# A shorter first transfer of wq: 2,048 of its columns instead of 4,096

## The chip, the cores and the metric

The kernel runs on one core of one Trainium2 chip. The time is device microseconds of one execution, taken as the median of several runs; lower is better. One further execution is recorded by the hardware profiler, and all profile lines come from that one.

## The reference

One decode step for two sequences: a layer norm, attention over the last 2,048 positions of a key and value cache, and a dense layer with a squared ReLU beside it, all added to the input.

```python
# x [2,1,576]; wq [576,4096]; wo [4096,576]; w1 [576,4608]; w2 [4608,576]; caches [2,16,8192,128]; bf16
xn = _layernorm(x)
# A: 32 query heads of 128 on 16 key/value heads, window W = 2048
q = (xn @ wq) -> [2,32,1,128]
scores = einsum("bhqd,bhkd->bhqk", q, k[:, :, Sk-W:]) * 128**-0.5
o = einsum("bhqk,bhkd->bhqd", softmax(scores), v[:, :, Sk-W:])
a = o.reshape(2, 1, 4096) @ wo
# B
h = relu(xn @ w1 + b1); b = (h * h) @ w2 + b2
return x + a + b
```

## The kernel before

**What is loaded.** About 53.6 MB come from HBM: wq (4.5 MiB), eight units of keys and eight of values (2 MiB each; a unit `u` is four key/value heads of one sequence), w1 (5,184 KB), wo (4,608 KB) and w2 in five pieces. All of them are issued from SyncE's queue (SP), in the order in which the program lists them. The biases, x and the output's first half are issued from ScalarE (ACT).

**The layout of the big weights.** `issue_flat` (L115) reads a weight as one flat row of numbers and gives each of the 128 partitions an equal, contiguous piece. For wq a piece is 18,432 columns: 9 blocks of `LQ` = 2,048, one block for each `t` in `range(NH)`, `NH` = 9. The tuple `cuts` says at which columns the load is cut into several transfers; all write the same tile. The before-kernel cuts wq at column 4,096 (L131), and so the first transfer holds the blocks t = 0 and 1, the second t = 2 to 8. A transfer is one stretch of memory on each of the 128 partitions: 8 KB and 28 KB per partition.

**The query projection.** `q_rows` (L232) runs over t = 0 to 8 and four column groups g, one matmul each (36 in all, recorded under L93, the helper `matmul`), into the PSUM tile `q_ps`. Block t of wq is needed by the four matmuls of t. `q_ps` is cleared by VectorE (DVE) first (L225), and the matmuls' other operand `xnT` comes out of the layer norm. `q_place` (L240) then copies `q_ps` to `qrow` (half on DVE, half on ACT), transposes it on TensorE (PE, `qT_ps`) and spreads it into `qz`.

**The units.** `transposes(u, g)` turns the keys on PE (recorded under L96) and copies them to `kT` (ACT and DVE in turn); `scores` multiplies `kT` with `qz`; `softmax(u)` follows. Keys and values share a pool of six buffers (`kvpool`), so a load of unit u waits until an earlier unit's buffer has been read. `step(u)` also does the value product `pv` of unit u - 2. The order of work on PE is that of the program (`keep_in_program_order`).

**The order of loads on SP.** wq (two transfers), k0, k1, v0, k2, v1, k3 ahead of everything; v2 after unit 0; k4 after step 1; then a k and a v per step, w1 after step 4; v6 and v7 after step 5. wo waits for the buffer `wbig`, which w1 holds until `mlp_h` (the dense layer's first half, L357) has read it; the five pieces of w2 (`w2a`, `w2b`, three into `w2c`) follow wo. The loads k2 and v1 also wait for an earlier transfer to have landed, as the wait table shows (SP L105 waits for wq twice, 8.0 us the longest).

**The end.** PE adds wo, w2a, w2b and w2c into `out_ps` as they land; three matmuls into `spin_ps` stand between w2b and w2c and are not read. `fin_sb` is copied out and stored from two queues.

Of the kernel before, what the change touches and what calls it, by code (L numbers as in the profile page):

```python
# [16 lines left out]
def kernel(  # L17
# [91 lines left out]
    def load_k(u):  # L109
        issue_kv(k_tiles, A_k_cache, u, "k")  # L110
# [4 lines left out]
    def issue_flat(w, name, cuts=()):  # L115
        n = w.shape[0] * w.shape[1] // P
        tl = wbig.tile([P, NH * L1], BF16, tag="wbig", name=name)
        w_p = w.rearrange("r n -> (r n)").rearrange("(p l) -> p l", p=P)
        for lo, hi in zip((0,) + cuts, cuts + (n,)):
            nc.sync.dma_start(out=tl[:, lo:hi], in_=w_p[:, lo:hi])  # L120
        return tl
# [6 lines left out]
    nc.vector.memset(eps_t[:], 1e-5)  # L128
    warm = const.tile([B, 2], F32, name="warm")
    nc.scalar.activation(out=warm[:, 0:1], in_=eps_t[:], func=ACT.Sqrt)  # L130
    wq_sb = issue_flat(A_wq, "wq", (4096,))  # L131
    load_k(0)
    load_k(1)
    load_v(0)
# [376 lines left out]
```

## Time and profile before

| what | value |
|---|---|
| time, median of 3 runs | 133.66 us (133.63 to 133.71) |
| time of the profiled execution | 133.6 us |
| its span, first to last instruction | 131.7 us |
| PE busy | 84.6 us (64%) |
| DVE busy | 63.1 us (48%) |
| ACT busy | 46.6 us (35%) |
| HBM read | 53.62 MB, 407 GB/s over the span |
| DMA queue of SP | 3,604 packets, 95.6% of 16 engines' span |
| mean granted TensorE clock | 0.883 |

The profile divides the span into 40 slices of 3.3 us; a digit is the busy share in tenths. A row of the chain of waits tells, followed back from the last instruction, what released each step; a DMA in it lasts from its issue to its landing, so time in which it stood in the queue behind other transfers is in its figure. A window row gives each engine's busy time in a stretch with the number of instructions, the granted PE clock (1.00 is full), the mean busy share of the 16 DMA engines, and GB/s. A packet's time is not cut exactly at a window's border, so a DMA share a little above 1 can stand there.

### The profile page before, as it was taken

To read this page: it belongs to the slowest core of one execution; us is meant where nothing else is said; L and a number is where in the kernel's file an instruction comes from. 1 tells how busy PE (TensorE), PEld (TensorE's weight loads), DVE (VectorE), ACT (ScalarE), POOL (GpSimd) and SP (SyncE) were. 2 spreads that over 40 slices of the span, in tenths; PEclk is the share of its full clock that TensorE was granted. 3 is DMA by queue.
4 is the path that set the end of the run, shared out by engine and by line. 5 is a ranking of instruction groups with operands and counts; after the bars stand their busy time and mean duration, and the time that the engine had idled before them with its cause. 6 is when DMAs were issued, how large, how long until landed. Compare 5 with 4: busy or idle time off the path is not lost.

```text
span 131.7 us, 2025 instructions
## 1 busy us (share of the span) xinstructions
PE 84.6 (64%) x818; PEld 46.3 (35%) x818; DVE 63.1 (48%) x176; ACT 46.6 (35%) x68; POOL 4.2 (3%) x14
## 2 busy tenths in 40 slices
PE   0040767985599687699687797003919974629782
PEld 0010236553346353345353353002507631205341
DVE  6760034555447677457677496400073487560000
ACT  6700019497255185265085283200015452000101
POOL 2000000010100100100100100100010001000000
PEclk9999999999779999859999999955586899655799
DMA  4999999999999999999999999999999989899970
GB/s 118 480 419 420 418 443 418 448 418 423 445 413 438 423 443 428 413 458 413 443 423 411 458 490 403 408 431 428 413 443 418 504 381 504 382 416 403 400 286 1
DMA packets 3643, 53.74 MB, mean 408 GB/s; under 512 B 418, under 2 KB 563, under 8 KB 819
## 3 DMA queue, kind: packets, MB, share of 16 engines
q1 hardware_dynamic: 3604, 53.61, 95.6%
q8 instruction: 6, 0.10, 0.3%
q10 hardware_dynamic: 30, 0.02, 0.0%
q14 instruction: 3, 0.02, 0.0%
HBM read 53.62 MB, written 0.00 MB: 407 GB/s over the span
## 4 chain that ended last, share of the span: by engine, by line
DMA 74%; PE 15%; ACT 5%; issue 1%; SPq 1%; DVE 1%; ACTq 0%; DVEq 0%
DMA w<-in_B_w_dram 24%; DMA w2c<-in_B_w_dram 23%; DMA k<-in_A_k_cache_dram 17%; DMA wq<-in_A_wq_dram 10%; PE kT_ps L96 5%; PE h_ps L93 3%; ACT kT L273 3%; PE q_ps L93 2%; PE sc_ps L93 2%; PE o_ps L93 1%; PE out_ps L93 1%; ACT L305 1%; SPq L120 1%; DVE qrow L241 1%; ACT qrow L241 0%
## 5 line engine op out<-in xcount | busy, mean ns | idle before, releaser
L96 PE MATMUL kT_ps<-ident_f,k 128*128 128x128 f32 x256 | 39.0, 295 | 6.7 <-DMA k<-in_A_k_cache_dram 4.2
L273 ACT COPY kT<-kT_ps 128x1024 bf16<-128x1024 bf16 x32 | 31.8, 1012 | 15.3 <-PE kT_ps L96 15.3
L96 PEld LDWEIGHTS kT_ps<-ident_f,k 128*128 128x128 f32 x256 | 29.3, 149 | 21.8 <-issue 7.4
L275 DVE COPY kT<-kT_ps 128x1024 bf16<-128x1024 bf16 x32 | 21.8, 682 | 6.4 <-PE kT_ps L96 5.9
L93 PE MATMUL sc_ps<-kT,qz 128*32 128x512 bf16 x128 | 9.8, 384 | 6.1 <-DVE kT L275 5.5
L305 ACT ACTIVATE p<-sc_ps,bias 128x512 bf16<-128x512 f32 x8 | 5.5, 687 | 21.5 <-DVE gown L301 21.4
L93 PE MATMUL o_ps<-v,pT 128*32 128x512 bf16 x128 | 12.2, 466 | 0.0
L93 PE MATMUL h_ps<-w,xnT 128*4 128x288 bf16 x72 | 4.5, 442 | 8.8 <-DMA w<-in_B_w_dram 8.8
L93 PEld LDWEIGHTS <-xnT 128*4 128x4 bf16 x108 | 3.5, 117 | 18.3 <-issue 15.3
L336 DVE SCALAR_TENSOR_TENSOR o<-o_ps,in_s,o 128x128 f32<-128x128 f32 x24 | 8.2, 344 | 0.4
L308 DVE STREAM_TRANSPOSE pT<-p 128x512 bf16<-128x512 bf16 x8 | 5.7, 709 | 5.6 <-ACT p L305 5.6
L376 DVE TENSOR_TENSOR hrow<-t 100x1152 bf16<-100x1152 f32 x2 | 2.6, 1354 | 10.5 <-ACT t L374 10.5
L93 PE MATMUL q_ps<-wq,xnT 128*4 128x512 bf16 x36 | 4.2, 622 | 5.4 <-DMA wq<-in_A_wq_dram 4.0
L294 DVE TENSOR_REDUCE m<-sc_ps 128x1 f32<-128x512 f32 x8 | 5.5, 691 | 3.4 <-PE sc_ps L93 3.4
L93 PE MATMUL op_ps<-o,of_h 128*32 128x129 f32 x16 | 3.4, 299 | 4.6 <-DVE o L336 4.6
L298 POOL PARTITION_ALL_REDUCE gmax<-m x8 | 2.9, 365 | 92.2 <-DVE m L296 92.2
L93 PEld LDWEIGHTS <-qz 128*32 128x32 bf16 x128 | 2.0, 94 | 9.9 <-DVE kT L275 7.6
L334 DVE TENSOR_SCALAR o<-o_ps,in_s 128x128 f32<-128x128 f32 x8 | 2.7, 343 | 5.3 <-PE o_ps L93 5.3
L96 PE MATMUL pro_ps<-ident,xn_sb 2*128 2x2 bf16 x5 | 0.9, 181 | 6.8 <-DVE xn_sb L171 6.5
L241 ACT CAST qrow<-q_ps 100x512 bf16<-100x512 f32 x1 | 0.6, 585 | 12.1 <-DVE qrow L241 12.1
L463 ACT COPY pre_sb<-pre_ps 34x288 f32<-34x288 f32 x1 | 0.4, 393 | 12.6 <-PE pre_ps L93 12.6
L93 PE MATMUL out_ps<-wo,ws 128*2 128x288 bf16 x32 | 4.0, 441 | 1.1 <-DVE ws L352 1.1
(76 smaller groups left out, 61.4 us busy)
## 6 DMA issues: line engine op xcount, KB each, us to landing
k<-in_A_k_cache_dram SPq DMA_DIRECT2D x8, 2048.0 KB, 25.6
v<-in_A_v_cache_dram SPq DMA_DIRECT2D x8, 2048.0 KB, 22.8
w<-in_B_w_dram SPq DMA_DIRECT2D x1, 5184.0 KB
wo<-in_A_wo_dram SPq DMA_DIRECT2D x1, 4608.0 KB
wq<-in_A_wq_dram SPq DMA_DIRECT2D x1, 3584.0 KB, 12.9
w2a<-in_B_w_dram SPq DMA_DIRECT2D x1, 2592.0 KB
w2b<-in_B_w_dram SPq DMA_DIRECT2D x1, 1296.0 KB, 29.2
wq<-in_A_wq_dram SPq DMA_DIRECT2D x1, 1024.0 KB, 4.8
```

Of the source, the lines that this page charges most:

```text
L93: tc.keep_in_program_order(nc.tensor.matmul(*a, **k))
L96: tc.keep_in_program_order(nc.tensor.transpose(*a, **k))
L241: cp(out=qrow[:, k * QW:(k + 1) * QW].rearrange("p (i a d) -> p i a d", a=2, d=Dh), in_=q_ps[0:RB, k * QW // 2:(k + 1) * QW // 2].rearrang ...
L273: nc.scalar.copy(out=kT, in_=kT_ps[:])
L275: nc.vector.tensor_copy(out=kT, in_=kT_ps[:])
L294: nc.vector.tensor_reduce(out=m1[:], in_=sc_ps[:], axis=AX.X, op=ALU.max)
L298: nc.gpsimd.partition_all_reduce(gmax[:], m2[:], channels=P, reduce_op=ReduceOp.max)
L305: nc.scalar.activation(out=p_sb[:], in_=sc_ps[:], func=ACT.Exp, bias=bias[:, 0:1], scale=scale, accum_out=o1[:, Dh:Dh + 1])
L308: nc.vector.transpose(out=pT[:].rearrange("p j r -> p (j r)"), in_=p_sb[:])
L334: nc.vector.tensor_scalar(scalar1=in_s[:, 0:1], scalar2=None, op0=ALU.mult, **kw)
L336: nc.vector.scalar_tensor_tensor(scalar=in_s[:, k:k + 1], in1=o1[:, 0:Dh], op0=ALU.mult, op1=ALU.add, **kw)
L376: nc.vector.tensor_tensor(out=h4[:, :, k * HB:(k + 1) * HB], in0=t4, in1=t4, op=ALU.mult)
```

## The change

One number: the column at which wq's load is cut.

```diff
     warm = const.tile([B, 2], F32, name="warm")
     nc.scalar.activation(out=warm[:, 0:1], in_=eps_t[:], func=ACT.Sqrt)
-    wq_sb = issue_flat(A_wq, "wq", (4096,))
+    wq_sb = issue_flat(A_wq, "wq", (2048,))
     load_k(0)
     load_k(1)
```

The first transfer is 128 x 2,048 elements (512 KB, 4 KB per partition) and the second 128 x 16,384 (4,096 KB, 32 KB per partition). The number of transfers, their order on SP and every instruction of the other engines are the same in both kernels; what each matmul of `q_rows` has to wait for is not.

## The prediction

> **What bounds the kernel now.** I read the slices first, to see whether any engine is full all the time:
>
> ```profile
> PE   0040767985599687699687797003919974629782
> DMA  4999999999999999999999999999999989899970
> GB/s 118 480 419 420 418 443 418 448 418 423 445 413 438 423 443 428 413 458 413 443 423 411 458 490 403 408 431 428 413 443 418 504 381 504 382 416 403 400 286 1
> ```
>
> The 16 DMA engines are full from the second slice to the last but two; PE has holes everywhere. Next the chain of waits, of which these are the long pieces (start us, length us, what):
>
> ```profile
> 1.18 12.89 DMA wq<-in_A_wq_dram
> 14.08 0.04 issue
> 14.12 3.18 PE q_ps L93 x28
> ...
> 31.95 22.43 DMA k<-in_A_k_cache_dram
> ...
> 59.41 31.63 DMA w<-in_B_w_dram
> ...
> 96.95 30.81 DMA w2c<-in_B_w_dram
> 127.75 0.04 issue
> 127.80 1.36 PE out_ps L93 x18
> ```
>
> The chain names `q_ps`, but the three later DMA pieces are queue time. The key load issued at 31.95 moves 2 MiB, which at the 431 GB/s shown below takes 2.097/0.431 = 4.9 us, and lands after 22.4: for more than 17 us it stood behind others. So what lies ahead of 31.95 in this chain need not set the end. What sets it is the sum of bytes, from the start of the flow (about 2.5 us) to the last landing near 128, and then 1.4 us of PE and the store.
>
> Last the projection itself on PE (timeline), then the unit after which PE is first held up again by a load:
>
> ```profile
> 9.10 1.02 PE L93 MATMUL q_ps<-wq,xnT 128*4 128x512 bf16 x8 [1.37 <-DVE q_ps L225]
> 14.12 3.16 PE L93 MATMUL q_ps<-wq,xnT 128*4 128x512 bf16 x28 [4.00 <-DMA wq<-in_A_wq_dram]
> ...
> 35.05 1.97 PE L96 MATMUL kT_ps<-ident_f,k 128*128 128x128 f32 x8 [1.52 <-DMA k<-in_A_k_cache_dram]
> ```
>
> The first 8 matmuls (t = 0 and 1) wait for DVE's clearing of `q_ps`, not for wq, whose first transfer landed 4.8 us after its issue at 0.73, near 5.5. The other 28 wait 4.0 us for the second transfer. At 35.05 PE has been idle for 1.52 us until k2 landed.
>
> **The change part by part.**
>
> *Matmuls moved behind the second landing.* The first transfer now holds t = 0 alone: 4 matmuls run at 9.10, and 32 instead of 28 after 14.08. The row gives 3.18/28 = 0.114 us each, so 4 more are 0.45 us. `q_ps` is complete near 17.75 instead of 17.30, and `qrow`, `qz`, unit 0 and unit 1 follow that much later. What hides it: PE's 1.52 us of idle before k2, which shrinks to about 1.07. Late behind it are two loads that wait for buffers: v2 (issued at 24.19) and k4 (31.95). Ahead of v2 the queue holds wq and six units, 4.72 + 6 x 2.097 = 17.3 MB, which at 0.431 MB per us from 2.5 us on last until 42.6. So 18 us of cover stand against 0.45. Later loads have similar cover: no load of values took less than 19.9 us from issue to landing for its own 4.9. The last that waits for PE is wo, issued at 95.62 after the dense layer; that layer starts on w1's landing (91.04, PE idle for 8.8 us ahead of it), and k7, v6, v7 still stand behind w1, 3 x 4.9 us, so until about 105.7. Cost on the end: 0. If the cover were gone: 0.45.
>
> *The bytes at another cut.* Both kernels move the same bytes in the same number of rows. The trace has no 4 KB row, so I take the rate per busy share (GB/s divided by the DMA share) from windows in which one row length rules:
>
> ```profile
> core 0: us, PE busy (x) PEld busy (x) DVE busy (x) ACT busy (x) POOL busy (x), PEclk, DMA share, GB/s
> 3.50:4.50 1.00, 0.00 (x0) 0.00 (x0) 1.00 (x5) 0.97 (x3) 0.00 (x0) 1.00 1.03 434
> 7.00:13.00 6.00, 1.57 (x11) 0.53 (x12) 1.58 (x7) 0.00 (x0) 0.00 (x0) 1.00 1.02 441
> 20.00:60.00 40.00, 32.21 (x267) 18.82 (x265) 23.22 (x54) 22.30 (x31) 1.46 (x4) 0.91 1.01 431
> 82.00:90.00 8.00, 0.25 (x2) 0.08 (x1) 1.76 (x5) 0.78 (x2) 0.36 (x1) 0.75 0.94 402
> 127.40:128.00 0.60, 0.45 (x6) 0.17 (x5) 0.00 (x0) 0.00 (x0) 0.00 (x0) 1.00 0.42 162
> ```
>
> wq's 8 KB rows: 434/1.03 = 421. Its 28 KB rows: 441/1.02 = 432. w1's 40.5 KB rows: 402/0.94 = 428. The last pieces of w2c, rows of 2.25 and 1.125 KB (288 and 144 KB over 128 partitions): 162/0.42 = 386. Before, wq costs 1.049/0.421 + 3.670/0.432 = 2.49 + 8.50 = 10.99 us. After, 0.524 MB at 386 to 421 is 1.36 to 1.25, and 4.194 MB at 432 (32 KB lies between 28 and 40.5) is 9.71: together 10.96 to 11.07. That is -0.03 to +0.08; 4 KB stands about midway between the two ends, and I take +0.02.
>
> *The start of the flow.* Before the first byte lands, a packet of each engine is under way; a row of 8 KB on each of 16 engines is 131 KB, 0.31 us at 421, and one of 4 KB half that. If the first row has to be read whole before it is written, the flow starts 0.15 us earlier: -0.15 to 0. Against it: the first transfer drains 0.524/0.421 = 1.25 us earlier, and the second must be ready by then. From windows of half a microsecond the DMA share is 0.37 at 2.0 to 2.5, 0.73 to 3.0 and 0.93 to 3.5, so transfers issued at 0.73 flow after some 1.3 to 2.3 us. The second is issued at about 1.15 and would flow from 2.4 to 3.4; the first now ends near 5.1 - 1.25 = 3.85. So the queue does not run dry, with 0.4 us in hand. If it did, the ramp would be lost again: 0.5 x (0.63 + 0.27 + 0.07) = 0.48 us. So -0.15 to +0.48; nearest to the rows is no bubble and a part of the gain, and I take -0.05.
>
> A rule of the Trainium skill speaks against the shorter transfer: DMA: Bandwidth & Descriptors, Rules for kernel authors, asks for at least 1 MiB per DMA for full bandwidth, and the new first one has half that. The same page's fit of a DMA, about 2.0 us plus its bytes at 436 GB/s, would by an estimate put the landing of 1 MiB at 4.4 us (the trace has 4.8) and of 512 KB at 3.2, and leave the sum of two transfers as it was, since there are two before and after. What would let the rule bite is the bubble, a rival below.
>
> *Queue of SP.* Two issues of wq before and after (0.86 us for both). k2's issue, now at 5.59, follows the first transfer's landing and comes some 1.2 us earlier; v1's (14.09) follows the second's landing and stays. Behind both lie k0, k1 and v0, 6.3 MB or 14.6 us, so no engine sees the difference: 0.
>
> *Sum.* 0 + 0.02 - 0.05 + 0 = -0.03 us against the profiled execution's 133.6 (span 131.7, 1.9 around it), which stands 0.06 under the median. Forecast: 133.65, no change. Its own range is -0.18 to +0.13, about 133.5 to 133.8.
>
> **Rivals.**
>
> 1 (slower). *The late queries go through.* The 0.45 us would reach the end if one resynchronising wait were missing: PE's 1.52 us before k2 and 8.8 us before the dense layer. At the end PE is only just ahead of the loads: it waits 0.25 us for w2a, 0.21 for w2b and 0.15 for w2c, so a lag of 0.45 that lived until there would show nearly whole. Price: 133.66 + 0.45 = 134.1. For it: the chain of waits runs through `q_ps`. Against it: both waits, each longer than 0.45. It decides as soon as less than 0.45 us of the wait for k2 is left.
>
> 2 (slower). *A bubble at the start.* The second transfer isn't flowing when the first has drained. Price 0.48: 134.1. For it: only 0.4 us in hand, by a ramp read from coarse windows. Against it: the seam between the two transfers at 5 us, with the same two issues 0.4 us apart, shows no dip below the mean that the next slice doesn't return.
>
> 3 (faster, or slower). *Another finish of the 16 engines.* They don't end together: over 126 to 128 us the DMA share is 0.68 where it was 0.97 just before, so some are done while the last still work; 0.32 x 2 = 0.64 us of it is unevenness. Different first rows shift the engines against each other at the start and what they meet later (instruction fetches are in the queue table). Half of that, 0.32, either way: 133.3 or 134.0. For it: the end hangs on the slowest engine alone. Against it: each engine gets the same bytes as before.
>
> 4. *The edit does nothing at all.* Excluded as a separate case: the two transfers do change size; it gives the forecast's time.
>
> **How the numbers follow.** Forecast 0.56, which includes the whole of a start gain of 0.15. Rival 1: 0.12. Rival 2: 0.08. Rival 3: 0.16 faster, 0.08 slower. A change under 0.2% (0.27 us) is about what a measurement of this kernel can tell from no change. So faster 0.16, same 0.56, slower 0.28. The range reaches from rival 3's gain to rivals 1 and 2: 133.3 to 134.15, with tails of rival 3 beyond it.
>
> **What would show it.** Right: 4 matmuls of `q_ps` near 9.1 and 32 from about 14.1; `qrow` near 17.8; a wait for k2 near 1.1 us that ends at 35.05 as before; the DMA share unbroken between 3 and 5 us; w2c's landing at 127.7 within 0.2. Wrong: a DMA share that falls between 3.5 and 4.5 us (rival 2); k2, w1 or w2c landing at their old times but PE later at the end (rival 1); w2c landing earlier or later while the start looks the same (rival 3). A second transfer that lands much before or after 14.08 would show that the price by rate is wrong.

## The result and the profile after

The changed kernel takes 133.91 us (median of 21 runs, 133.49 to 134.2) against 133.64 us for the kernel before (21 runs, 133.47 to 133.8). The ratio is 1.0016, with a 95% interval of 1.0010 to 1.0022: slower by a quarter of a microsecond, inside the forecast's range, but a change where none was forecast. Its runs also scatter more, over 0.71 us against 0.33.

The profiled execution of the changed kernel took 134.15 us (span 132.3), near the top of that scatter; the profile of before took 133.6. So the two traces differ by 0.55 us, about twice what the medians differ by.

First the slices of the changed kernel (busy tenths in 40 slices, and GB/s):

```profile
PE   0040579997697597497598787104729971649572
...
DMA  4999999999999999999999999999999999899960
GB/s 107 488 408 428 402 451 421 436 431 431 419 426 436 421 436 426 436 431 426 431 419 436 431 483 414 419 449 387 441 426 441 468 435 457 364 426 423 405 237 1
```

The picture is that of before: the DMA engines are full from the second slice on, PE has holes. Next the long pieces of its chain of waits (start us, length us, what):

```profile
1.19 13.39 DMA wq<-in_A_wq_dram
14.58 0.04 issue
14.63 3.61 PE q_ps L93 x32
...
33.36 21.21 DMA k<-in_A_k_cache_dram
...
58.09 33.02 DMA w<-in_B_w_dram
...
96.59 31.69 DMA w2c<-in_B_w_dram
128.28 0.04 issue
128.33 1.37 PE out_ps L93 x18
```

wq's second transfer lands at 1.19 + 13.39 = 14.58 us, where it was 14.07; the large piece of w2c lands at 128.28, where it was 127.76. The difference is 0.51 at the first place and 0.52 at the last, so the loss seems to arise in the first 14 us, while the same 4.5 MiB of wq came in, and to stay until the end. (The two figures belong to different DMA engines, as the explanation below shows.) PE's own work after the last landing is 1.37 us, as before.

The projection on PE, and the first wait for a load behind it (timeline of PE):

```profile
9.10 0.60 PE L93 MATMUL q_ps<-wq,xnT 128*4 128x512 bf16 x4 [1.37 <-DVE q_ps L225]
14.63 3.58 PE L93 MATMUL q_ps<-wq,xnT 128*4 128x512 bf16 x32 [4.92 <-DMA wq<-in_A_wq_dram]
...
35.30 1.09 PE L96 MATMUL kT_ps<-ident_f,k 128*128 128x128 f32 x8 [0.36 <-DMA k<-in_A_k_cache_dram]
```

4 matmuls are early and 32 late, as forecast, and the wait for k2 has shrunk from 1.52 us to 0.36, although the landing that ends it is itself 0.25 later. So PE is 1.41 us late here: 0.51 by wq's landing, 0.45 by the 4 moved matmuls, and 0.45 between the projection and this point.

### The profile page after: what moved, and what is told of

It reads as the page before. It is cut to its first block, busy times and chain, and to the rows that moved or that the text cites. A ratio compares the mean times of both kernels' runs of the same rounds, so it can differ in the third digit from the quotient of the medians.

```text
span 132.3 us, 2025 instructions
## 1 busy us (share of the span) xinstructions
PE 83.6 (63%) x818; PEld 47.5 (36%) x818; DVE 63.2 (48%) x176; ACT 46.8 (35%) x68; POOL 4.2 (3%) x14
## 4 chain that ended last, share of the span: by engine, by line
DMA 75%; PE 16%; ACT 4%; SPq 2%; issue 1%; DVE 1%; ACTq 0%
DMA w<-in_B_w_dram 25%; DMA w2c<-in_B_w_dram 24%; DMA k<-in_A_k_cache_dram 16%; DMA wq<-in_A_wq_dram 10%; PE kT_ps L96 6%; PE h_ps L93 3%; PE q_ps L93 3%; ACT kT L273 2%; PE sc_ps L93 2%; PE out_ps L93 1%; ACT L305 1%; PE qT_ps L96 1%; PE o_ps L93 1%; SPq L120 1%; DVE qrow L241 1%
## 5 line engine op out<-in xcount | busy, mean ns | idle before, releaser
L96 PEld LDWEIGHTS kT_ps<-ident_f,k 128*128 128x128 f32 x256 | 30.2, 151 | 20.4 <-issue 12.1
L93 PE MATMUL o_ps<-v,pT 128*32 128x512 bf16 x128 | 11.2, 429 | 0.0
L241 DVE CAST qrow<-q_ps 100x512 bf16<-100x512 f32 x1 | 0.7, 691 | 9.2 <-PE q_ps L93 9.2
```

What stands on the lines that cost most here:

```text
L93: tc.keep_in_program_order(nc.tensor.matmul(*a, **k))
L96: tc.keep_in_program_order(nc.tensor.transpose(*a, **k))
L241: cp(out=qrow[:, k * QW:(k + 1) * QW].rearrange("p (i a d) -> p i a d", a=2, d=Dh), in_=q_ps[0:RB, k * QW // 2:(k + 1) * QW // 2].rearrang ...
```

## The experiments

The windows of the changed kernel's start come first (columns as in the prediction's). The flow doesn't stop between its two transfers:

```profile
core 0: us, PE busy (x) PEld busy (x) DVE busy (x) ACT busy (x) POOL busy (x), PEclk, DMA share, GB/s
2.00:2.50 0.50, 0.00 (x0) 0.00 (x0) 0.43 (x3) 0.50 (x1) 0.00 (x0) 1.00 0.69 90
2.50:3.00 0.50, 0.00 (x0) 0.00 (x0) 0.47 (x3) 0.48 (x3) 0.00 (x0) 1.00 0.72 238
3.00:3.50 0.50, 0.00 (x0) 0.00 (x0) 0.50 (x4) 0.50 (x1) 0.00 (x0) 1.00 1.27 459
3.50:4.00 0.50, 0.00 (x0) 0.00 (x0) 0.50 (x2) 0.50 (x1) 0.00 (x0) 1.00 1.98 778
4.00:4.50 0.50, 0.00 (x0) 0.00 (x0) 0.50 (x4) 0.47 (x3) 0.00 (x0) 1.00 0.96 410
```

The DMA share is 1.27, 1.98 and 0.96 from 3.0 to 4.5 us (a packet's bytes aren't cut at the window's border, so it goes above 1). No window shows a queue run dry, and the trace's records of single packets agree: from 2.5 to 13 us never fewer than 16 are under way. (A packet is one row, the stretch that one DMA engine writes to one partition.) They also show rows that took too long. These are the first rows of the second transfer (start us, end us, bytes, ns):

```
3.485  4.698  32768  1213
3.563  5.743  32768  2180
3.602  4.815  32768  1213
3.678  4.891  32768  1213
```

An undisturbed 32 KB row takes 1,213 ns, and one engine's first row of this transfer took 2,180. Slow first rows stand in every kernel of this study, but none of the others has a row after 3.3 us that is so far over its usual time; in the kernel before the worst between 3.3 and 14 us is a row of 8 KB that took 486 ns instead of 309. So the question was whether single engines' lags at the start set the end, or PE's later projection, or the row sizes as such.

### The changed kernel again

No edit.

> The changed kernel once more, beside the others on one chip. It lost 0.16% (133.91 against 133.64 us), and in its profile the second transfer of wq landed at 14.58 us instead of 14.08, of which one packet that stood for about 2.2 us explains most. Theory A (short rows at the start: the 16 DMA engines lose time while the flow begins, and the 4 KB rows lose more of it than 8 KB rows): again +0.1 to 0.25%, second transfer of wq lands 0.2 to 0.6 us later than before's 14.08. Theory B (the 4 matmuls of t = 1 behind the second landing): the same +0.2%, but the landing at 14.1. Theory C (nothing but the scatter between runs): within 0.05%.

Measured: 133.77 us against 133.6, ratio 1.0009 (1.0000 to 1.0017). Its profile took 133.85 us, and wq's second transfer landed at 1.18 + 13.07 = 14.25. The sign holds, the size is about half of the first measurement; the landing is late by 0.18 and the profiled time by 0.25.

### The first transfer at 1,024 columns

```diff
-    wq_sb = issue_flat(A_wq, "wq", (4096,))
+    wq_sb = issue_flat(A_wq, "wq", (1024,))
```

> The first transfer is 1,024 columns, 2 KB rows; the second has 34 KB rows and all 36 matmuls of the projection stand behind it (0.9 us later than in the kernel before). Theory A: the loss grows or stays, +0.2 to 0.5% (133.9 to 134.3 us), wq lands at 14.4 to 15. Theory B: twice the changed kernel's loss, +0.3 to 0.4% (134.1), with wq landing at 14.1. Theory C: 133.65 within 0.1.

Measured: 133.63 us against 133.6, ratio 0.9997 (0.9989 to 1.0006), landing at 14.21. Theory A, by which shorter rows lose more, misses: 2 KB rows lose nothing that is measured. Theory B misses too, with all 36 matmuls late.

### The first transfer at 8,192 columns

```diff
-    wq_sb = issue_flat(A_wq, "wq", (4096,))
+    wq_sb = issue_flat(A_wq, "wq", (8192,))
```

> The first transfer is 8,192 columns, 16 KB rows; t = 0 to 3 can run on it, so 16 matmuls are early and 20 late (0.9 us earlier than in the kernel before). Theory A: no loss, 133.5 to 133.65, wq lands at 13.8 to 14.1. Theory B: 0.2 to 0.4% faster, 133.1 to 133.4. Theory C: 133.65 within 0.1.

Measured: 133.66 us, ratio 1.0004 (0.9996 to 1.0013). 16 early matmuls gain nothing: theory B misses again. The profiled execution, at 133.88, is the slowest of its eleven.

### Only PE late, no transfer altered

```diff
-        for t in range(NH):
+        for t in (2, 0, 1, 3, 4, 5, 6, 7, 8):
...
-                       rhs=wq_sb[:, o:o + QW], start=(t == 0), stop=(t == NH - 1), skip_group_check=True,
+                       rhs=wq_sb[:, o:o + QW], start=(t == 2), stop=(t == NH - 1), skip_group_check=True,
```

> The cut of the kernel before (4,096 columns), but the matmuls of q_rows in the order t = 2, 0, 1, 3 to 8, so that all 36 stand behind the second landing: the projection ends 8 x 0.114 = 0.9 us later, twice the change's part, and no transfer is altered. Theory A: the time of before, 133.65 within 0.1, wq lands at 14.1. Theory B: +0.3 to 0.9 us, 134.0 to 134.5. Theory C: 133.65 within 0.1.

Measured: 133.6 us, ratio 1.0003 (0.9994 to 1.0012). PE's timeline of this kernel:

```profile
14.33 4.01 PE L93 MATMUL q_ps<-wq,xnT 128*4 128x512 bf16 x36 [6.60 <-DMA wq<-in_A_wq_dram]
...
34.81 1.09 PE L96 MATMUL kT_ps<-ident_f,k 128*128 128x128 f32 x8 [0.20 <-DMA k<-in_A_k_cache_dram]
```

All 36 matmuls stand behind the landing, twice the change's delay, and the wait for k2 still isn't used up (0.20 us left). The late projection costs nothing that shows (by the interval at most 0.12%, 0.16 us). This is the part of the forecast that holds.

### Cuts around the changed one, and the two sizes in the other order

```diff
-    wq_sb = issue_flat(A_wq, "wq", (4096,))
+    wq_sb = issue_flat(A_wq, "wq", (1536,))
```

The other three have 2560, 3072 and 16384 in its place.

> First transfer 1,536 columns (3 KB rows), second 33 KB rows; all 36 matmuls late as in the cut at 1,024, which measured 133.63 us. Theory A2 (what costs is the begin of the flow with rows of about 4 KB: each engine has several rows in hand before the first bytes come, and one engine falls behind): 133.7 to 133.9, wq's second landing later than 14.2. Theory D (only 4 KB + 32 KB, both round powers of two, are bad: the size or address itself): 133.6, landing at 14.1. Theory C (scatter): 133.6, any landing.

> First transfer 2,560 columns (5 KB rows), second 31 KB rows; PE's order and waits as in the changed kernel (4 matmuls early, 32 late). Theory A2: 133.7 to 133.9. Theory D: 133.6. Theory B is no longer held, since 36 late matmuls (0.9 us) measured 133.60.

> First transfer 3,072 columns (6 KB rows), second 30 KB rows; PE as in the changed kernel. Theory A2: between the changed kernel and the one before, 133.65 to 133.75. Theory D: 133.6.

> The changed kernel's two sizes in the other order: first 16,384 columns (32 KB rows), then 2,048 (4 KB rows). 32 matmuls can run on the first transfer. The flow begins on long rows and the 4 KB rows come in its middle. Theory A2: the time of before, 133.5 to 133.65. Theory D, if the sizes themselves cost: 133.75 to 133.9.

Measured against 133.49 us of before in these runs: 1,536 columns 133.59, ratio 1.0008 (0.9999 to 1.0017); 2,560 columns 133.68, 1.0022 (1.0010 to 1.0033); 3,072 columns 133.59, 1.0010 (1.0001 to 1.0019); 16,384 columns 133.84, 1.0023 (1.0013 to 1.0033). Theory A2 fits 2,560 and 3,072, but not 16,384, where the flow begins on 32 KB rows and loses as much; theory D fits 16,384, but not 2,560. No rule by row length covers all of them.

What goes with the times better is the landing. In this table the last transfer of wq, the 864 KB piece of w2c and the time are from one profiled execution each; "before" stands for the cut at 4,096. The landings are issue plus length in the chain of waits (for 8,192 and 16,384, whose chain doesn't hold that transfer, from the longest issue-to-landing time of wq's tile, so to 0.1). The executions are not all from one session; the kernel before had medians of 133.49 to 133.64 us beside them.

| kernel | wq all landed, us | w2c landed, us | difference | time of that execution, us |
|---|---|---|---|---|
| cut 1,536 | 14.03 | 127.75 | 113.72 | 133.59 |
| cut 3,072 | 14.03 | 127.77 | 113.74 | 133.61 |
| before | 14.07 | 127.76 | 113.69 | 133.6 |
| before's cut, PE late | 14.20 | 127.77 | 113.57 | 133.6 |
| cut 1,024 | 14.21 | 127.81 | 113.60 | 133.68 |
| cut 8,192 | 14.2 | 128.03 | 113.8 | 133.88 |
| cut 2,048, again | 14.25 | 127.98 | 113.73 | 133.85 |
| cut 2,560 | 14.31 | 127.99 | 113.68 | 133.84 |
| cut 16,384 | 14.4 | 128.04 | 113.6 | 133.86 |
| cut 2,048 (after) | 14.58 | 128.28 | 113.70 | 134.15 |

The landing of wq ranges over 0.55 us, the time over 0.56, and the stretch between wq's landing and w2c's over some 0.25. Theory G, which the next four kernels were made to test, reads it so: the engine that leaves the start last carries its lag through 113.7 us of full queue to the end. The table fits that only in the large. Four kernels landed wq between 14.20 and 14.25 us, and their executions took 133.6 to 133.88; one of them, with only PE late, issues the very transfers of before, landed wq 0.13 later and took the same time.

### The start of the flow given to another load

```diff
-    wq_sb = issue_flat(A_wq, "wq", (4096,))
     load_k(0)
+    wq_sb = issue_flat(A_wq, "wq", (4096,))
     load_k(1)
```

The second of the pair has 2048 in place of 4096.

> k0 is loaded ahead of wq, with the cut of the kernel before: the flow begins on 16 KB rows, wq comes 4.9 us later in its middle, and so does all of PE's first work. It is the partner of the next kernel. Theory G (what costs is where the flow begins: the engine that leaves the start last carries its lag to the end, and the kernel's time follows it one for one): within 0.15 us of the kernel before if PE's 4.9 us are caught up, 133.5 to 133.9. Theory B2 (PE's lateness counts once it is over the 1.5 us of idle before k2): 135 or more.

> k0 ahead of wq, with the cut at 2,048: the 4 KB rows come in the middle of the flow. Theory G: equal to lead4096 within 0.1 us, the changed kernel's loss of 0.1 to 0.3 us is gone. Theory D (the sizes 4 KB and 32 KB cost wherever they stand): 0.15 to 0.3 us over lead4096.

Measured, against 133.51 us of before: 133.84 us (ratio 1.0029, 1.0018 to 1.0041) with the cut at 4,096 and 133.85 (1.0026, 1.0015 to 1.0037) at 2,048. The chains of waits of the two, first 4,096, then 2,048:

```profile
2.05 17.11 DMA wq<-in_A_wq_dram
...
96.98 30.98 DMA w2c<-in_B_w_dram
```

```profile
2.04 17.11 DMA wq<-in_A_wq_dram
...
97.00 30.89 DMA w2c<-in_B_w_dram
```

wq is all there at 19.16 and 19.15 us: with the start out of the way, the cut makes no difference to the landing, nor to the time. It isn't hidden behind a lag of k0's either: averaged over the 16 DMA engines, wq is done at 18.59 and 18.60 us. Both are 0.3 us over the kernel before; by the landing less k0's 4.9 us, the start on k0's rows lost 0.2 us against the start on wq cut at 4,096. PE's projection begins 5 us later in both, which costs 0.3 us at the very most; the 135 of theory B2 is far off.

### A small transfer ahead

```diff
-    wq_sb = issue_flat(A_wq, "wq", (4096,))
+    wq_sb = issue_flat(A_wq, "wq", (256, 4096))
```

The other has (256, 2048).

> Three transfers of wq, cut at 256 and 4,096 columns: rows of 512 B first (64 KB in all), then 7.5 KB and 28 KB. Theory G with cold rows (an engine's first rows wait for their first bytes one after another, and short ones get that over with little data in hand): wq's last landing at 13.9 to 14.2 us, 133.4 to 133.6. If a short row costs as such: 133.7 to 133.9, landing later than 14.2.

> Three transfers, cut at 256 and 2,048 columns: 512 B rows, 3.5 KB rows, 32 KB rows. Theory G with cold rows: as warm256 within 0.1 us. If short rows at the start cost as such: 0.1 to 0.4 us over warm256, with wq's last landing as much later.

Measured: 134.0 us (ratio 1.0039, 1.0026 to 1.0051) and 134.02 (1.0045, 1.0032 to 1.0057). The chain of waits of the first has

```profile
1.65 12.85 DMA wq<-in_A_wq_dram
```

so wq is all there at 14.50 us, and at 14.54 in the other; their profiled times are 134.04 and 134.01. The hope that a few short rows get the first waits over with little data in hand is wrong: both starts are 0.4 us worse. The relation of the table holds for them within 0.2 us (113.55 and 113.51 from wq's landing to w2c's), and the cut at 2,048 adds nothing measurable to the cut at 4,096 here.

## Why the prediction was wrong

**Late matmuls: right.** 4 at 9.10 and 32 from 14.63 in 3.58 us, 0.11 us each; cost on the end 0, shown by the kernel in which only PE is late. The wait for k2 came out at 0.36 us and not 1.1, in part because the landing of wq was late as well (the 1.41 us of PE's lateness above; what made its last 0.45 was not followed).

**The bytes at another cut: right.** In the trace's packet records an undisturbed 4 KB row takes 159 ns where 8 KB takes 309, 28 KB 1,062 and 32 KB 1,213. Eight of each per engine give 8 x (159 + 1,213) = 10.98 us after and 8 x (309 + 1,062) = 10.97 before: +0.01, where +0.02 was taken. The prediction had named a second landing away from 14.08 as the sign that this price is wrong. The sign came, but the price was not its reason.

**The queue of SP: right in effect.** k2 was issued at 4.83 us and not 1.2 us earlier than 5.59, since the first transfer landed later than forecast (4.1 us after its issue, where 4.8 - 1.25 = 3.55 would follow from its bytes). So a lag is there by the end of the first transfer. With 1,024 columns k2's issue is at 3.59, and nothing is lost.

**The start of the flow: the step that failed.** It was given -0.15 to +0.48, and -0.05 was taken, with "no bubble and a part of the gain". The profiles show +0.51 and +0.18 for the landing of wq, and the medians +0.27 and +0.17 us. The sum's own range, -0.18 to +0.13, also left out the +0.48 that this term had been given; with it the upper end would have been +0.56. It was not the bubble of rival 2 either: the size of 0.48 fits the first profile, but the queue didn't run dry. In its place stands a lag of single DMA engines. The sum treated 16 engines as one pipe of 430 GB/s, in which a lag of one engine is worth a sixteenth. But each engine works off its own share of every transfer, eight rows of wq's second one, and a transfer has landed when the last of them is done. By the mean over the 16 engines the start cost only 0.16 and 0.07 us (on average an engine is done with wq at 13.69 and 13.60 us, where it was 13.53 before); the rest is unevenness. Rival 3 had the mechanism: uneven engines, shifted by other first rows against each other and against the instruction fetches that they meet later. It put that at 0.32 us either way, with chance 0.16 for the gain and 0.08 for the loss, and the loss came. Nothing in the trace of before told which of the two it would be.

How the lag reaches the end can be followed in the packet records. They don't name the engine, but on one engine a row begins within a few ns of the end of the one before, so its rows can be strung together. These are three engines (the end of the last row of each transfer, us; w2a and the 864 KB piece of w2c are pieces of w2):

| engine | wq, first transfer | wq, second | instruction packet | w1 | w2a | 864 KB piece of w2c |
|---|---|---|---|---|---|---|
| before: last of all, at wq and at the end | 5.24 | 13.72 | 28.92 to 29.88 | 90.59 | 122.21 | 127.38 |
| after: with the row of 2,180 ns, last at wq | 3.56 | 14.21 | none | 89.66 | 121.28 | not last |
| after: last at the end | 4.45 | 14.13 | 105.53 to 106.42 | 89.58 | 122.64 | 127.81 |

From wq to w1 an engine that nothing else interrupts takes 75.45 us, in both kernels, to within a few ns: an engine keeps the lag of the start, and nothing behind it takes it away. But the queue table also lists six packets of 16 KB for instructions (q8), and each comes to another engine, between two rows of a load, and makes that engine about 1.4 us later (76.87 instead of 75.45 in the first line). Two packets of 8 KB (q14) cost two more engines 0.55 and 0.84 us in the kernel before. So six engines stand behind the ten others, and the last of these six sets the end. The engine with the row of 2,180 ns set the landing of wq and not the end: it met no such packet. The one that set the end was late by the end of the first transfer: 4.45 us, where 5.24 less 8 x (309 - 159) ns = 1.20 would be 4.04. At the end of wq it was just as much, 14.13 - 13.72 = 0.41, behind the one that set the end before. That is 0.41 of the 0.52 us by which w2c landed later. In the second profile of the changed kernel the engine that set the end was 0.16 late at both places (4.20 and 13.88 us), of 0.22 by which w2c landed later.

In all fourteen traces the engine that ends last has met one of the six packets. In two of them, before and the cut at 8,192, it is also the one that ended wq last; in the other twelve it ended wq up to 0.23 us ahead of the last one. With wq at the front, the four traces in which it was furthest ahead (0.15 to 0.23 us) have the shortest stretches from wq's landing to w2c's, 113.51 to 113.60. So theory G is right that a lag is carried to the end, and wrong that the engine last at wq decides. The landing of wq goes with the time to within some 0.25 us because one of the six was always close to the last.

That the loss comes from the start and not from the cut as such is shown by the pair in which another load takes the start and the cut no longer matters. Windows of the tail agree. These are the last 3 us of transfers in the changed kernel:

```profile
126.00:127.00 1.00, 0.73 (x12) 0.53 (x13) 0.00 (x0) 0.00 (x0) 0.00 (x0) 1.00 0.95 377
127.00:128.00 1.00, 1.00 (x13) 0.51 (x8) 0.00 (x0) 0.00 (x0) 0.00 (x0) 1.00 0.50 193
128.00:129.00 1.00, 0.86 (x13) 0.50 (x12) 0.00 (x0) 0.00 (x0) 0.00 (x0) 1.00 0.20 74
```

and of before:

```profile
126.00:127.00 1.00, 1.00 (x19) 0.67 (x14) 0.00 (x0) 0.00 (x0) 0.00 (x0) 1.00 0.92 362
127.00:128.00 1.00, 0.84 (x7) 0.33 (x7) 0.00 (x0) 0.00 (x0) 0.00 (x0) 1.00 0.44 168
128.00:129.00 1.00, 1.00 (x18) 0.64 (x14) 0.00 (x0) 0.00 (x0) 0.00 (x0) 1.00 0.12 43
```

In both the DMA share halves at 127 us, and only a few engines still work; after the change they work longer (0.50 and 0.20 of the last two microseconds where it was 0.44 and 0.12).

What stays open is why an engine's first rows stand, and why the cut at 4,096 has the quiet start: 1,024 columns start as well as 4,096 by their medians, 2,560 and 16,384 badly, and no single quantity of the cut orders them. With one profile for each kernel (two for the changed one), which engine is hit can't be told from chance. That the instruction packets make the late engines is read from the traces; no kernel was tried without them. The rule of the Trainium skill that was weighed (DMA: Bandwidth & Descriptors, Rules for kernel authors: at least 1 MiB per DMA) has the sign of the changed kernel, but not of the others: a first transfer of 256 KB measured 0.9997, and one of 4 MiB with 512 KB behind it 1.0023. The fit of the Trainium skill that the prediction quotes from the same page is given there for DMAs issued from GpSimd, and these are issued from SP; its estimates of 4.4 and 3.2 us for the two first landings stand against 4.8 in the trace of before and 4.1 and 3.8 in those of the changed kernel.

No kernel of the study is measurably faster than the one before.

## What to carry to other kernels

In a kernel that keeps its DMA queue full from start to end, nothing takes a lag off a DMA engine again that it picks up in the first microseconds, and it counts at the end if that engine is among the late ones there. The landing of the first big transfer shows the largest such lag, and its change told the change of the end to about 0.25 us here. Sum such a kernel by its latest DMA engine, not by mean GB/s: 16 equal shares finish as late as the last of them, and that is an engine which had something else to do as well, here an instruction packet of about 1.4 us. A difference of 0.1 to 0.3 us between two such kernels can then rest on which engine was late, so one profile of each doesn't explain it. PE's work, which looked critical in the chain of waits because it was followed through queue time, could be moved by 0.9 us at no cost, so ask of each DMA in the chain how much of its length is its own bytes.

## What was not expected of the hardware

The 16 engines end the same transfer far apart. By the packet records of before, ten of them write their last row of w1 between 88.76 and 89.15 us, and the last one at 90.59; in the changed kernel the last one is at 90.77. The four latest of before (90.20 to 90.59) are those that had met an instruction packet by then. A 16 KB row of a load takes its engine 611 ns, and a 16 KB instruction packet makes it 1.4 us later. In these traces a lag at the start therefore counts only on the six engines that meet such packets. That would explain why the same kernel scatters over 0.7 us, but single executions other than the profiled ones have no packet records to show it.

The rows themselves are very even once the flow runs: 611 ns for 16 KB, 1,364 for 36 KB and 1,533 for 40.5 KB, within a few ns except beside an instruction packet. So nearly all of the spread between the kernels comes from the first microseconds and from the engines that the instruction packets meet.
